# The first four blocks of a dynamic convolution and squared-ReLU network: 128-token chunks in block 0, and a new written order of the steps in blocks 0 to 3

## The chip, the cores and the metric

The kernel runs on one core of one Trainium2 chip. The metric is the device time of one execution in microseconds (us), from the first to the last instruction of that core. Lower is better.

## What is computed

The inputs are x (8 batches, 4096 tokens, 192 channels), weight_gen (for each token, 8 heads and 7 taps), and the two matrices w_in (192 x 2048) and w_out (2048 x 192) of a feed-forward network. The core of the reference is:

```python
w = softmax(weight_gen, over the 7 taps)
x_pad = 6 zero tokens ahead of each batch, then x
out[b, s, h, g] = sum over k of w[b, s, h, k] * x_pad[b, s + k, h, g]   # 24 channels g per head
h = maximum(out.reshape(32768, 192) @ w_in, 0)
result = (h * h) @ w_out
```

## The kernel before

**Blocks.** The 32768 tokens are 64 sub-blocks of 512 tokens. Blocks 0 and 1 hold one sub-block each, blocks 2 to 32 hold two. The two halves of a block, for one sub-block each 256 tokens, use the upper and the lower 64 rows of the TensorE array: 192 channels are three slices of 64.

**The steps.** In the code and in this text they have short names:
- *Softmax* (L131 to L235): a part of a batch's weights is loaded (`load`, L173), ACT takes the exponent (`exp`, L195), DVE sums over taps, takes the reciprocal and multiplies (L202, L209, L217), giving v. Small parts (8 tokens per partition) go to `v_first`, the others to `v_big`. `move_rows` then copies v's rows by DMAs from SP and POOL into `wr` tiles (L308), one small DMA for each of five token tiles; later parts go through DRAM (`vd`).
- *Band* (`st_band`, L326): DVE multiplies the rows with a mask, which gives for each of five token tiles a banded matrix `bd`.
- *Conv* (`st_conv`, "C"): TensorE multiplies x with the bands (L394, tiles of 32 columns of the array) into PSUM tiles `yp`; ACT copies them as fp16 into `y` (L405). The order of the matmuls comes from `conv_pieces`.
- *Unit* (`st_unit`, "u"): 12 matmuls of 64x256 (blocks 0 and 1, two slices of 128 hidden features) or 6 of 64x512 into one PSUM tile `h` (L419); ACT takes the ReLU into `t1` (L428), DVE squares it into `g` (L431). Block 0 and 1 have 8 units, the others 16.
- *Second matmul* ("M", `st_mm2`, L453): one M is half of the hidden features (8 of 16 chunks) for a quarter of 256 tokens. It sums in the PSUM banks `o`. After a quarter's second M, ACT copies `o` to `o_sb` (L467); where two banks were used (quarters of block 2 and later), DVE adds the second bank (L469). SP stores two quarters at a time (L474).

**What sets the order.** The program order is written by hand, and each engine runs its own instructions in that order. For each block a string gives the order on TensorE (`orders`, L558): block 0 "uuuuuCuuu", block 1 "MuMuuuMuuuMCu", block 2 "MuuuuMuuuuMuuuuuuuMCu", then `steady`, three times "MuMuuu" and then "MuuuMCu". The M steps in block j belong to block j - 1, C is the conv of block j + 1. Exponents, the rest of the softmax, bands and loads are hung on units by a table (`fill`, `TIMES`, `at`), and run just ahead of the unit (`run_fill`). x of blocks 2 and on is loaded by POOL (`x_load`) at the end of a block.

**Pools.** The PSUM tiles of conv, units and the warm-up share three buffers (`ps_h`); the `o` banks have one buffer each (`ps_o`). There are five `t1`, so the sixth ReLU waits for the first square. x has two fp16 buffers, bands three, rows four.

**The opening** (L506 to L554). TensorE spins on 42 warm-up matmuls. SP loads the first weights, w_in's two halves (`w_st`) and x of block 0 (`x_st`). ACT and DVE make the first softmax, and ACT casts w_in and x. SP and POOL move rows for block 0 (token tiles in the order 0, 2, 1, 4, 3, on the two in turn) and POOL those of block 1. `cross_w_in` copies each half of w_in across partitions by two SP DMAs (L126). Then follow x of block 1, the load of the second softmax part (s1), the bands of block 0, conv(0), the bands of block 1, and the cast of x(1) on DVE. A one-element POOL memset on `x_st` (L550) stands ahead of POOL's four loads of w_out (`load_w_out`, L139), so that these wait until x(1) has been cast; behind them stand the load of s2 and a memset of `v_big` (L554).

Of the kernel before, what the change touches and what calls it, by code (L numbers as in the profile page):

```python
# [9 lines left out]
def kernel(  # L10
# [7 lines left out]
):  # L18

# [279 lines left out]
    def wr_load_sbuf(j, parts, order, engines):  # L299

        wr_t[j] = p_wr.tile([P, NT, HP, SL * 2], f16, name="wr")
        n = 0
        for i in order:
            t0 = max(j % NBB * TB + tile_start(j, i), 0)
            for s in parts:
                a, b = max(t0, s.t0), min(t0 + P, s.t0 + P * s.r)
                if a < b:
                    engines[n % len(engines)].dma_start(  # L308
                        out=wr_t[j][a - t0 : b - t0, i].rearrange("p g c -> p (g c)"),
                        in_=s.v[  # L310
                            (a - s.t0) // s.r : (b - s.t0) // s.r, HALO : HALO + s.r
                        ].rearrange("p r g c e -> p r (g c e)"),
                    )
                    n += 1
# [33 lines left out]
    def conv_pieces(j):  # L348


        s0, n = BLOCKS[j]
        th = n * TB // 2
        halves = []
        for half in (0, 1):
            s, a = (s0 + half, 0) if n == 2 else (s0, th * half)
            halves.append([
                (s, i, half, max(bounds[i], a), min(bounds[i + 1], a + th), a)
                for i in range(NT) if bounds[i] < a + th and bounds[i + 1] > a
            ])
        if n == 2:  # L360
            for k in range(NK):
                for later in (True, False):
                    for pair in zip(*halves):
                        for s, i, half, a, b, base in pair:
                            for q in (2 * k, 2 * k + 1):
                                yield later, s, i, q, half, a, b, base
        else:
            for pair in zip(*halves):
                for later in (True, False):
                    for k in range(NK):  # L370
                        for s, i, half, a, b, base in pair:
                            for q in (2 * k, 2 * k + 1):
                                yield later, s, i, q, half, a, b, base

    def st_conv(j):

        n = BLOCKS[j][1]
        th = n * TB // 2
        per = 1024 // th
        y = p_y.tile([P, NK, TB], f16, name="y")  # L380
        y_t[j] = y
        yps = [
            ps_h.tile([P, 2 * TB], f32, name="yp", tag="h") for _ in range(-(-NK // per))
        ]
        for later, s, i, q, half, a, b, base in conv_pieces(j):
            lo = bounds[i]
            hi = lo + (STEP if tile_start(s, i) == starts[i] else bounds[i + 1] - lo)
            _, ha, hb, pre = quads[q]
            m, h = (32, hb) if later else (pre, ha)
            bd = bd_t[s][:, H * lo : H * hi].rearrange("p (g c e) -> p g e c", g=HP, e=2)  # L390
            p0 = RT * half + 32 * (q % 2)
            k = q // 2
            col = th * (k % per) - base
            nc.tensor.matmul(  # L394
                out=yps[k // per][p0 : p0 + m, col + a : col + b],
                lhsT=x_t[s][:, i, 32 * q : 32 * q + m],
                rhs=bd[:, h // 2, h % 2, a - lo : b - lo],
                start=True,
                stop=True,
                skip_group_check=True,  # L400
                tile_position=(0, p0),
            )
        for n, yp in enumerate(yps):
            k0, k1 = n * per, min((n + 1) * per, NK)
            nc.scalar.copy(  # L405
                out=y[:, k0:k1, 0:th],
                in_=yp[:, 0 : (k1 - k0) * th].rearrange("p (k c) -> p k c", c=th),
            )

    def st_unit(j, u):  # L410

        th = BLOCKS[j][1] * TB // 2
        per = TB // th
        h = ps_h.tile([P, 2, TB], f32, name="h", tag="h")
        for jj in range(per):
            for slot in range(NK):
                for half, r0 in enumerate((0, RT)):
                    k = slot ^ half if slot < 2 else slot
                    nc.tensor.matmul(  # L419
                        out=h[:, half, jj * th : (jj + 1) * th],  # L420
                        lhsT=w_in_chunk(u * per + jj, slot, half),
                        rhs=y_t[j][r0 : r0 + RT, k, 0:th],
# [7 lines left out]
        g_t[(j, u)] = g  # L430
# [4 lines left out]
    def new_o(pool, banks=2):  # L435
        if pool is ps_o:
            return [ps_o.tile([P, TB], f32, name=f"o{i}") for i in range(banks)]
# [3 lines left out]
    def st_mm2(j, qt, fcs, ccs, o):  # L441


        th = BLOCKS[j][1] * TB // 2
        per = TB // th
        half, off = divmod(qt * QT, th)
        for fc in fcs:
            g = g_t[(j, fc // per)][:, half, fc % per * th + off :]
            for cc in ccs:
                n = P // len(o)  # L450
                for i, oo in enumerate(o):
# [3 lines left out]
                        lhsT=g[r0 : r0 + n, cc * P : (cc + 1) * P],  # L455
# [32 lines left out]
    with nc.allow_low_precision("fp16 matmul pipeline"), tc.manual_schedule():  # L488
# [32 lines left out]
        spin(42)  # L521
        band_mask()
# [13 lines left out]
        wr_load_sbuf(0, [s0], (0, 2, 1, 4, 3), (nc.sync, nc.gpsimd))  # L536
        wr_load_sbuf(1, [s0], range(NT), (nc.gpsimd,))
        cross_w_in(0)
        x_cast(0, nc.scalar.copy)
        x_load_f32(1)  # L540
# [3 lines left out]
        for i in (0, 2, 1, 3, 4):  # L544
            st_band(0, (i,))
        st_conv(0)
        st_bands(1)
        x_cast(1, nc.vector.tensor_copy)

        nc.gpsimd.memset(x_st[1][:, 0:1], 0.0)  # L550
# [3 lines left out]
        nc.gpsimd.memset(v_big, 0.0)  # L554
# [3 lines left out]
        orders = {0: "uuuuuCuuu", 1: "MuMuuuMuuuMCu", 2: "MuuuuMuuuuMuuuuuuuMCu"}  # L558
        steady = "MuMuuu" * 3 + "MuuuMCu"

# [4 lines left out]
        def at(j, u, kind, *args):  # L565
# [5 lines left out]
            (0, 2): ((1, 7), (2, 0)),  # L571
            (0, 3): ((2, 15), (3, 0)),
# [8 lines left out]
        def exp_time(j, u):  # L581

            if u == 0:
                return j - 1, 5 if j == 2 else 12
            return j, {1: 0, 7: 3, 9: 4, 15: 8}[u]

        at(0, 4, "exp", s1, 0, s1.rh)
        at(0, 5, "soft", s1, 0, s1.rh)
        for n, s in enumerate(parts[2:], 2):
# [5 lines left out]
            pieces = [(lo, min(lo + PIECE, s.rh)) for lo in range(0, s.rh, PIECE)]  # L595
            for (j, u), (lo, hi) in zip(times, pieces, strict=True):
                at(*exp_time(j, u), "exp", s, lo, hi)
                at(j, u, "soft", s, lo, hi)
            if n > 2:
                at(times[0][0] - 1, 0, "load", s)  # L600
        for j in range(1, NBLK - 1):
            a = BLOCKS[j + 1][0]
            small = [p for p in parts if p.fb <= j + 1][-1].r == FIRST
            us = {1: (1, 3), 2: (6, 8), 6: (7, 9)}.get(j, (5, 9) if small else (1, 5))
            for n, u in enumerate(us):
                at(j, u, "band", a + n)
# [14 lines left out]
        def run_fill(j, u):  # L621
            for kind, *args in fill.get((j, u), ()):
                if kind == "band":
                    st_bands(*args)
                    continue
                if kind == "load":
                    args[0].load(nc.sync)
                    continue
                s, lo, hi = args
                if kind == "exp":  # L630
                    s.exp(lo, hi)
                    continue
                s.total(lo, hi)
                s.recip(lo, hi)
                s.scale(lo, hi, nc.vector)
                if hi < s.rh:
                    continue
                if s.r == FIRST:
                    move_rows(s)
                    after = parts[parts.index(s) + 1]  # L640
                    if after.b == s.b and after.r > FIRST:
                        s.store(nc.sync)
                else:
                    s.store(nc.sync)
                    stored.add(s)
                    for w in [w for w in waiting if w[0] is s]:
                        waiting.remove(w)
                        load_rows(w[1])

        FCS = (range(NF // 2), range(NF // 2, NF))  # L650
        for j, (sub, n) in enumerate(BLOCKS):
            if j + 2 < NBLK:
                load_rows(j + 2)
            u = m = 0
            for step in orders.get(j, steady):
                if step == "M":
                    qt, part = divmod(m, 2)
                    m += 1
                    if part == 0:
                        o = new_o(ps_o, 1 if j < 3 else 2)  # L660
                    st_mm2(j - 1, qt, FCS[part], (0, 1), o)
                    if part == 1:
                        o_sum(j - 1, qt, (0, 1), o)
                        if qt % 2:
                            o_store(j - 1, qt - 1, range(4), nc.sync)
                elif step == "u":
                    run_fill(j, u)
                    st_unit(j, u)
                    u += 1
                elif j + 1 < NBLK:  # L670
                    st_conv(j + 1)
            if j == 0:
                x_load(2)
                x_load(3)
            elif j < NBLK - 2:
                for k in range(BLOCKS[j + 2][0], sum(BLOCKS[j + 2])):
                    x_load(k)
# [47 lines left out]
```

The softmax here doesn't subtract the row's maximum and nothing guards it: scores larger than these inputs give would overflow.

## Time and profile before

| | |
|---|---|
| three runs | 749.04, 749.24 and 750.09 us, median 749.24 |
| span of the profiled execution | 749.2 us, granted clock 1.000 |
| ReLU, `t<-h` (L428) | 512 times, 1027 ns each on ACT |
| square, `g<-t` (L431) | 512 times, 687 ns each on DVE |
| second matmul (L453) | 8032 matmuls |
| units (L419) | 3168 matmuls |
| a block of 1024 tokens in the steady part | 22.55 us |
| w_out DMAs (L139) | four, from 18.75 us, 5.4 us each from issue to landing |
| load of s1 (L173) | issued by SP at 14.39 us |

A row of the profile's order of time reads: start in us, duration in us, engine, line, operation, output and input with their sizes, how many times; in brackets the idle time of the engine just before, and who ended it. A row with a count merges neighbours of one kind. A row of busy time by stretches reads: the stretch, its length, and for PE (matmuls), PEld (weight loads), DVE, ACT and POOL the busy us with the number of instructions; then the granted clock, the share of time that the DMA engines were busy (overlapping packets can take it over 1) and GB/s. SPq, ACTq and POOLq are queues' issue times of DMAs.

### The profile page before, as it was taken

What the parts mean: (1) busy time and instruction counts of PE and PEld (TensorE: products, weight loads), DVE (VectorE), ACT (ScalarE), POOL (GpSimd) and SP (SyncE); (2) the same over time, 40 slices, a digit from 0 to 9 for tenths busy, and PEclk for the clock granted to TensorE, in tenths of its full rate; (3) what the DMA queues carried; (4) which work ended last, traced back from release to release, by engine and by line L of the source; (5) the groups of instructions that cost most, each with busy time, mean ns of one, the idle gap of its engine ahead of it and who ended that gap; (6) DMA issues with size and microseconds to landing.
All of it is one profiled execution on the core that took longest, in us unless ns stands there. A gap on an engine that the chain in (4) does not pass through costs nothing.

```text
span 749.2 us, 33282 instructions
## 1 busy us (share of the span) xinstructions
PE 739.0 (99%) x15106; PEld 559.8 (75%) x15106; DVE 621.8 (83%) x1001; ACT 623.0 (83%) x753; POOL 87.9 (12%) x127
## 2 busy tenths in 40 slices
PE   8899999999999999999999999999999999999998
PEld 4658777777887777777877777777778777777787
DVE  5889998998789888887888888898888987677853
ACT  4898888888888888888888888888888888888883
POOL 3522220001101000011000110001100011001000
PEclk9999999999999999999999999999999999999999
DMA  8846444446453344543245442365441354441312
GB/s 231 129 74 135 79 68 109 101 78 138 93 109 69 74 77 80 131 86 65 46 80 139 86 80 49 55 138 108 59 79 47 57 109 80 59 75 50 50 45 65
DMA packets 122329, 65.20 MB, mean 87 GB/s; under 512 B 83881, under 2 KB 118668, under 8 KB 121676
## 3 DMA queue, kind: packets, MB, share of 16 engines
q1 hardware_dynamic: 77868, 46.05, 22.4%
q0 software_dynamic: 44176, 16.93, 20.6%
q8 instruction: 118, 1.93, 1.1%
q14 instruction: 23, 0.19, 0.1%
q10 hardware_dynamic: 144, 0.10, 0.0%
HBM read 48.61 MB, written 28.70 MB: 103 GB/s over the span
## 4 chain that ended last, share of the span: by engine, by line
PE 88%; DVE 5%; DMA 3%; ACT 1%; issue 1%; SPq 0%; POOL 0%; DVEq 0%; ACTq 0%
PE o L453 42%; PE h L419 40%; PE yp L394 6%; DVE g L431 2%; DVE bd L326 1%; DMA xt<-in_x_dram 1%; ACT t L428 1%; DMA x_st<-in_x_dram 1%; DMA vd<-v_big 1%; DVE v_first L217 1%; DVE ssum L202 0%; DVE rcp L209 0%; DMA wg<-in_weight_gen_dram 0%; DVE o_sb L469 0%; POOL wr L308 0%
## 5 line engine op out<-in xcount | busy, mean ns | idle before, releaser
L428 ACT ACTIVATE t<-h 128x1024 f16<-128x1024 f32 x512 | 497.1, 1027 | 66.9 <-PE h L419 66.6
L431 DVE TENSOR_TENSOR g<-t 128x1024 f16<-128x1024 f16 x512 | 334.5, 687 | 101.9 <-ACT t L428 99.1
L453 PEld LDWEIGHTS <-g 64*128 64x128 f16 (+1 forms) x8032 | 353.0, 94 | 55.7 <-issue 5.0
L453 PE MATMUL o<-w_o,g 64*128 64x192 f16 (+1 forms) x8032 | 386.1, 243 | 1.7 <-DMA w_o<-in_moe_w_out_dram 0.7
L419 PE MATMUL h<-y,w_i 64*128 64x512 f16 (+1 forms) x3168 | 379.8, 370 | 2.1 <-ACT t L428 0.9
L419 PEld LDWEIGHTS <-w_i 64*128 64x128 f16 x3168 | 165.5, 94 | 114.7 <-issue 5.0
L326 DVE TENSOR_TENSOR bd<-wr,mask 128x4160 f16<-128x4160 f16 (+3 forms) x89 | 149.4, 1702 | 4.6 <-DMA wr<-v_first 4.6
L278 POOL DMA_DIRECT2D xt<-in_x_dram x62 | 51.3, 832 | 446.1 <-PE yp L394 422.8
L467 ACT COPY o_sb<-o 128x384 f32<-128x384 f32 x129 | 62.3, 483 | 33.2 <-PE o L453 33.2
L469 DVE TENSOR_TENSOR o_sb<-o,o_sb 128x384 f32<-128x384 f32 x123 | 68.2, 554 | 8.0 <-ACT o_sb L467 5.6
L405 ACT CAST y<-yp 128x1024 f16<-128x1024 f32 (+1 forms) x64 | 48.2, 803 | 16.5 <-PE yp L394 16.5
L394 PE MATMUL yp<-bd,xt 128*32 128x104 f16 (+8 forms) x3864 | 52.0, 208 | 1.8 <-DMA xt<-in_x_dram 1.2
L394 PEld LDWEIGHTS <-xt 128*32 128x32 f16 (+3 forms) x3864 | 46.1, 91 | 8.0 <-issue 6.4
L217 DVE TENSOR_TENSOR v_big<-ex,rcp 128x112 f16<-128x112 f32 (+1 forms) x136 | 27.3, 263 | 1.8 <-DMA vd<-v_big 0.6
L195 ACT ACTIVATE ex<-wg 128x448 f32<-128x448 f32 (+2 forms) x44 | 27.2, 618 | 1.9 <-DMA wg<-in_weight_gen_dram 1.9
L202 DVE TENSOR_REDUCE ssum<-ex 128x64 f32<-128x448 f32 (+2 forms) x44 | 26.1, 593 | 2.4 <-ACT ex L195 2.4
L209 DVE RECIPROCAL rcp<-ssum 128x64 f32<-128x64 f32 (+2 forms) x44 | 23.7, 539 | 1.5
L268 POOL DMA_DIRECT2D xt<-in_x_dram x7 | 3.8, 547 | 136.9 <-PE yp L394 136.9
L308 POOL DMA_DIRECT2D wr<-v_first x31 | 16.8, 562 | 15.4 <-DVE v_first L217 15.3
L516 PE MATMUL wp<-warm 128*128 128x512 f16 x42 | 11.1, 432 | 1.3 <-DVE warm L508 1.3
L516 PEld LDWEIGHTS <-warm 128*128 128x128 f16 x42 | 4.5, 109 | 7.4 <-issue 2.5
L217 DVE TENSOR_TENSOR v_first<-ex,rcp 128x112 f16<-128x112 f32 (+1 forms) x48 | 9.1, 255 | 0.3
(19 smaller groups left out, 24.5 us busy)
## 6 DMA issues: line engine op xcount, KB each, us to landing
out_dram<-o_sb SPq DMA_DIRECT2D x63, 384.0 KB, 2.9
xt<-in_x_dram POOLq DMA_DIRECT2D x42, 240.0 KB, 6.0
wg<-in_weight_gen_dram SPq DMA_DIRECT2D x4, 1064.0 KB, 7.7
xt<-in_x_dram POOLq DMA_DIRECT2D x20, 192.0 KB, 5.6
wr<-vd SPq DMA_DIRECT2D x38, 80.0 KB, 5.0
vd<-v_big SPq DMA_DIRECT2D x5, 512.0 KB, 5.5
wg<-in_weight_gen_dram SPq DMA_DIRECT2D x5, 392.0 KB, 4.2
wg<-in_weight_gen_dram SPq DMA_DIRECT2D x3, 616.0 KB, 5.5
```

Source lines behind the costliest of these rows:

```text
L195: nc.scalar.activation(out=self.ex[:, lo:hi].rearrange("p r g k e -> p (r g) k e"), in_=self.wg[:, lo:hi].rearrange("p r (g e) k -> p (r g ...
L217: eng.tensor_tensor(out=bass.AP(tensor=v.tensor, offset=v.offset + lo * H * SL + lo % SL * 2 + g * SL * 2, ap=[list(v.ap[0]), [H * SL + 2, ...
L278: eng.dma_start(out=dst[:, first:last], in_=ap)
L326: nc.vector.tensor_tensor(out=bd_t[j][:, H * lo : H * (lo + len(tiles) * n)].rearrange("p (g m c) -> p g m c", g=shape[1], c=2 * SL), in0= ...
L394: nc.tensor.matmul(out=yps[k // per][p0 : p0 + m, col + a : col + b], lhsT=x_t[s][:, i, 32 * q : 32 * q + m], rhs=bd[:, h // 2, h % 2, a - ...
L405: nc.scalar.copy(out=y[:, k0:k1, 0:th], in_=yp[:, 0 : (k1 - k0) * th].rearrange("p (k c) -> p k c", c=th),)
L419: nc.tensor.matmul(out=h[:, half, jj * th : (jj + 1) * th], lhsT=w_in_chunk(u * per + jj, slot, half), rhs=y_t[j][r0 : r0 + RT, k, 0:th], ...
L428: nc.scalar.activation(out=t1, in_=h, func=ActF.Relu)
L431: nc.vector.tensor_tensor(out=g, in0=t1, in1=t1, op=AluOp.mult)
L453: nc.tensor.matmul(out=oo[:, cc * Dm : (cc + 1) * Dm], lhsT=g[r0 : r0 + n, cc * P : (cc + 1) * P], rhs=w_o[r0 : r0 + n, fc, :], start=(fc ...
L467: nc.scalar.copy(out=o_sb, in_=o[0][:, c])
L469: nc.vector.tensor_tensor(out=o_sb, in0=o[1][:, c], in1=o_sb, op=AluOp.add)
```

## The change

- **Block 0 by chunks.** Its four chunks of 128 tokens go to the halves in turn: chunks 0 and 2 to the upper, 1 and 3 to the lower half (`place`, `spans`). Conv(0) has two parts of two chunks each, each with its own y copy of 128x384. Its first four units take one part only, and four slices of 128 features (`unit_span`): units 0 and 1 do features 0 to 1023 for part 0, units 2 and 3 for part 1, with 24 matmuls of 64x128 each. Units 4 to 7 are as before. Conv(0) has 96 matmuls instead of 72.
- **The opening.** The memset of `v_big` is POOL's first work. Rows of block 0 go in the order 0 to 4: tiles 0 to 2 on SP and POOL in turn, 3 and 4 on POOL. Rows of block 1: tiles 0 to 2 by ACT's queue, after the cast of x(0), 3 and 4 by POOL. Bands of block 0 are made in the order 0 to 4. The POOL memset on `x_st` is gone, so the loads of w_out and s2 follow the rows directly. x(2) is loaded right after conv(0)'s second part, x(3) right after conv(1).
- **The order of blocks 0 to 3** is written out with all kinds of steps: u, M, c (second part of conv(0)), C, B (bands of a sub-block), X (cast of x), E (one piece of an exponent), S (the rest of its softmax), L (load of a part). Blocks 4 and on keep `steady` and their table.
- **The banks.** M steps are numbered through by a generator, so they can stand in any block. For quarters of blocks 0 and 1, which use one bank, `o0` and `o1` now alternate.

```diff
+        nc.gpsimd.memset(v_big, 0.0)
         band_mask()
...
-        wr_load_sbuf(0, [s0], (0, 2, 1, 4, 3), (nc.sync, nc.gpsimd))
-        wr_load_sbuf(1, [s0], range(NT), (nc.gpsimd,))
+        wr_load_sbuf(0, [s0], (0, 1, 2), (nc.sync, nc.gpsimd))
+        wr_load_sbuf(0, [s0], (3, 4), (nc.gpsimd,))
         cross_w_in(0)
         x_cast(0, nc.scalar.copy)
+        wr_load_sbuf(1, [s0], (0, 1, 2), (nc.scalar,))
+        wr_load_sbuf(1, [s0], (3, 4), (nc.gpsimd,))
...
-        for i in (0, 2, 1, 3, 4):
+        for i in range(NT):
             st_band(0, (i,))
-        st_conv(0)
-        st_bands(1)
-        x_cast(1, nc.vector.tensor_copy)
-
-        nc.gpsimd.memset(x_st[1][:, 0:1], 0.0)
+        st_conv(0, 0)
         for q in range(4):
             load_w_out(q, 4)
         s2.load(nc.gpsimd)
-        nc.gpsimd.memset(v_big, 0.0)
-        orders = {0: "uuuuuCuuu", 1: "MuMuuuMuuuMCu", 2: "MuuuuMuuuuMuuuuuuuMCu"}
         steady = "MuMuuu" * 3 + "MuuuMCu"
+        plans = {
+            0: "B1 c u u u X1 u E1 S1 u u u M C u",
+            1: "L3 u B2 B3 u u u M u u E2 S2 M u E2 C S2 u M",
+            2: "L4 u u u E3 M u u u M B4 u u u u M B5 u u u S3 u M u E3 C u",
+            3: "L5 L6 M S3 u u u M u B6 u u E4 u M M B7 u u u u E4 M M u S4 C u M u u M u",
+        }
...
+    def unit_span(j, u):
+        if j == 0 and u < 4:
+            return range(u % 2 * 4, u % 2 * 4 + 4), u // 2 * P, P
...
-                        o = new_o(ps_o, 1 if j < 3 else 2)
+                    o = new_o(ps_o, 1, qt % 2) if j < 2 else new_o(ps_o)
...
+                elif kind == "c":
+                    st_conv(0, 1)
+                    x_load(2)
+                elif kind == "C" and j + 1 < NBLK:
+                    st_conv(j + 1)
+                    if j == 0:
+                        x_load(3)
```

## The prediction

> **What bounds the kernel now.** I read the page first, then the table of busy time by stretches, then the order of time of the first 62 us with its waits.
>
> ```profile
> PE 739.0 (99%) x15106; PEld 559.8 (75%) x15106; DVE 621.8 (83%) x1001; ACT 623.0 (83%) x753; POOL 87.9 (12%) x127
> ```
>
> TensorE looks full over the whole span, so only its stretches can tell where time is left. The next lines give, for each stretch, its length and the busy time of PE, PEld, DVE, ACT and POOL.
>
> ```profile
> 11.40:14.10 2.70, 2.21 (x55) 1.06 (x54) 2.60 (x5) 1.29 (x1) 1.05 (x3) 1.00 0.90 213
> 14.10:20.83 6.73, 5.75 (x167) 4.94 (x166) 5.51 (x7) 5.29 (x7) 2.18 (x4) 1.00 0.68 179
> 20.83:30.00 9.17, 7.45 (x108) 5.86 (x103) 7.06 (x17) 6.97 (x10) 7.84 (x11) 1.00 0.96 149
> 30.00:40.30 10.30, 9.06 (x222) 7.50 (x216) 9.35 (x16) 8.41 (x12) 2.86 (x5) 1.00 0.71 129
> 40.30:53.60 13.30, 13.02 (x122) 6.74 (x122) 11.88 (x18) 12.39 (x16) 3.11 (x6) 1.00 0.52 80
> 53.60:61.50 7.90, 7.90 (x224) 6.26 (x222) 7.76 (x18) 6.90 (x10) 2.23 (x3) 1.00 0.49 87
> 61.50:66.70 5.20, 5.06 (x88) 3.78 (x84) 3.86 (x10) 4.01 (x6) 2.72 (x5) 1.00 0.61 83
> 66.70:80.59 13.89, 13.89 (x315) 11.55 (x312) 13.39 (x19) 12.72 (x17) 0.29 (x1) 1.00 0.39 104
> 80.59:103.14 22.55, 22.55 (x476) 16.61 (x474) 21.77 (x43) 20.04 (x27) 4.74 (x9) 1.00 0.37 67
> ```
>
> From 80.59 us, the first second-matmul step of block 4, a block takes 22.55 us and PE has no idle time. Blocks 4 to 32 keep their order, so **what is won by 80.59 is won at the end, and no more**. Up to there no engine is full; the waits are these:
>
> ```profile
> 15.47 3.88 PE L419 MATMUL h<-y,w_i 64*128 64x256 f16 x60 [0.89 <-ACT y L405]
> 21.89 1.52 PE L419 MATMUL h<-y,w_i 64*128 64x256 f16 x24 [0.90 <-ACT t L428]
> 24.14 1.48 PE L453 MATMUL o<-w_o,g 128*128 128x192 f16 x16 [0.72 <-DMA w_o<-in_moe_w_out_dram]
> 36.65 1.58 PE L394 MATMUL yp<-bd,xt 128*32 128x104 f16 x118 [1.05 <-DMA xt<-in_x_dram]
> ...
> 14.57 2.36 DVE L326 TENSOR_TENSOR bd<-wr,mask 128x3328 f16<-128x3328 f16 x2 [0.48 <-DMA wr<-v_first]
> 17.47 0.66 DVE L292 CAST xt<-x_st 128x960 f16<-128x960 f32 x1 [0.54 <-DMA x_st<-in_x_dram]
> 21.87 0.69 DVE L431 TENSOR_TENSOR g<-t 128x1024 f16<-128x1024 f16 x1 [1.04 <-ACT t L428]
> 29.23 2.33 DVE L326 TENSOR_TENSOR bd<-wr,mask 128x4160 f16<-128x4160 f16 x1 [1.00 <-DMA wr<-v_first]
> 40.30 0.69 DVE L431 TENSOR_TENSOR g<-t 128x1024 f16<-128x1024 f16 x1 [0.88 <-ACT t L428]
> ```
>
> The bracket is idle time before the instruction. Three floors say how much there is to win by the first M of block 4:
> - **DVE**: its first band starts at 11.49; the eight stretches sum to 2.60+5.51+7.06+9.35+11.88+7.76+3.86+13.39 = 61.4 us busy. Floor 11.5+61.4 = 72.9.
> - **PE**: 48 units at 0.647 (18 matmuls, three units, in 1.94 in the chain of waits), 16 M at 1.32 (32 in 1.32 there), five convs about 6.2 (0.9, 0.9 and three near 1.5): 58.4. From 12.3: 70.7.
> - **ACT**: relus 0.915 apart (three in 2.85 with a tail of 1.02), so 48 cost 43.9; y copies about 6, o copies 8 x 0.48, exps about 4.3: 58. From a first copy at 13.8, plus 0.9 for the first unit: 72.7.
>
> So VectorE and ScalarE bound this stage nearly as closely as PE, and **DVE's 80.6 - 72.9 = 7.7 us of idle time is the sum to share out**.
>
> **What the Trainium skill says.** "TensorE: Matmul & The Clock Gate", section Back-to-back issue gap, gives N/2.4 + 2.5 ns warm, and a sustained 81 ns at N=128 with a weight load each. Our pairs of 512 columns agree with the first (1.94/9 = 216 ns). The second doesn't fit packed halves: 32 matmuls of 64x192 with 32 loads take 1.32, 41 ns each. The same page, Architectural detail, calls ACT and DVE strict FIFO: the waits above are all in program order, which agrees. "DMA: Bandwidth & Descriptors", Issuing engines are not separate DMA queues, says that SP, ACT and POOL issues share the same 16 DMA engines; its section on queues has an engine take rings in turn by packets. No run here shows how two queues share.
>
> **The change, part by part.**
> 1. *Conv of block 0 in two parts.* Part 0 needs bands 0 to 2 alone; the third band starts at 12.50 and takes 0.58. Its last 24 matmuls go out at 13.15 to 13.5, y copy (128x384, 0.48 as the o copy) at 13.8 to 14.3, against 14.62 to 15.42 now. Part 1 follows band 4 (ends 14.09), done about 14.5. First unit at 14.5, first relu about 15.3 instead of 16.34: **1.0 us earlier on ACT**. Added: 24 matmuls (13 ns each, 0.3, in PE's wait for bands) and about 0.2 of ACT copy.
> 2. *Four units of 24 matmuls x 128 columns in place of 12 x 256.* No such row before. Low end 12 pairs x 55.8 (skill) = 0.67, high end 24 x 41 (the 64x192 row; a narrower one is not dearer) = 0.99. ACT needs 0.915 per unit, so it hides the low end; the high end costs 0.3 + 4 x 0.08 = 0.6. I take 0.1.
> 3. *Rows of block 1.* Five DMAs leave SP's and POOL's queues for three on ACT and two on POOL. Three ACT issues at 0.37 (ACT's one at the end) to 0.6 (SP's) take 9.6 to at most 11.5; behind them stands the second w_i cast, which waits for data until 11.22 anyway: 0 to 0.3, and it feeds only unit 4. SP is freed of one 0.6 issue, so x_st(1) leaves 0.6 sooner, and the 0.54 wait of its cast goes. POOL issues 5 instead of 7, so DVE's 0.48 wait goes.
> 4. *v_big memset* (2.5 us) to POOL's start: the mask is ready near 6.2, needed at 11.49; nothing. It leaves POOL's 22.3 to 24.8, where no one waited.
> 5. *w_o and s2 loads* lose the wait for x_st(1) (POOL idle 5.79) and follow five row issues: 11.4 instead of 18.75. The 0.72 wait on w_o goes. But 1.5 MB now runs beside the crossing of w_i (issued at 13.04, wanted by unit 4 near 18.9) and the s1 load (issued at 14.39). w_o's landing is 5.4 us, moving from about 1.7 after issue. The exp of s1 stands on ACT ahead of the fifth relu, wanted near 19.0. Low end: no delay. High end: the queues halve each other from 13 us on; what took HW transfers until 18.5 takes until 22, delay 3.0. Packets of the w_i and s1 transfers are far larger than w_o's, so turns by packet favour them: I take **0.8**.
> 6. *Order of block 0 and 1.* x(2) is loaded after conv part 1, x(3) after conv(1), behind POOL's five rows of S1, not at the end of the block (28.78): x(3) at about 26 to 27.6, landing near 33 by the 6 us in the issue table; conv(2) is wanted near 32. That ACT wait is absorbed, as DVE is then behind with S2. The first M moves into block 0. S1 now runs at 20 to 23.2 (0.96+0.85+1.46) instead of 22.5 to 25.8, its rows land 3.4 later (25.82 to 29.23 now), at 26.6, before DVE asks for bands 2 at 27: the 1.00 wait goes. The 0.21+1.04 before g of units 3 and 4 go, as bands and cast are ahead of them or hidden. First relu of block 2 comes near 37 instead of 41.2, so DVE's 0.88 goes too.
> 7. *Blocks 2 and 3.* The same steps, the same number of M by each block's start (4, 8, 16). The 3.5 us of DVE idle left there shrink where DVE carries a backlog: 0 to 2.0, I take 0.5. New waits: bands of block 6 follow S3 closely (0 to 1.0, take 0.5); block 3 ends "M u" and block 4 starts with M on the same two o banks, so PE waits for copy and sum (0.3+0.48+0.55) behind one unit of 0.65: 0 to 0.75, take 0.3, since part of it falls on DVE's wait. Alternating banks before that is free: M's there stand two or more units apart.
>
> Sum of removed DVE idle: 0.48+0.54+1.25+1.00+0.88 = 4.15; plus 0.5; minus 0.8, 0.5, 0.1, 0.3: **gain 2.95 us**. The profiled span is 749.2, the median of the runs 749.24: 746.2.
>
> **Rivals.**
> - *Nothing collides*: the w_o term is 0 and the backlog fills 2.0 of the later idle time: 4.15+2.0-0.9 = 5.2, 744.0. For it: HW transfers at 14 to 18 us ran at 160 to 350 GB/s, so they weren't always full.
> - *Collision*: delay 3.0 at the exp of s1, everything behind it on DVE (S1, bands 2 and 3) shifts: 2.95-2.2 = 0.75, 748.5.
> - *Given back*: block 3's bunched M M meet a DVE backlog; sums of o come late, PE waits on its banks; about 1.5 more lost: 747.7. For it: DVE is 21.77 of 22.55 full even in steady state.
> - *Slower*: the exp of s1 blocks ACT's queue. Break-even is where it starts 2.95+0.8 = 3.75 after 19.0, at 22.8; over 0.2% slower needs 24.3. At 25.5 the total is 751.9. Against it: that landing would take 10 us, the longest in the first 40 us is 6.5.
>
> **Chances.** My forecast (745 to 747.6) 0.45, nothing collides 0.22, given back 0.12 (half of it within 0.2%), collision 0.13, slower 0.08. Within 0.2% (1.5 us) is what a measurement here can't tell from no change. Faster 0.45+0.22+0.06 = 0.73, same 0.06+0.13 = 0.19, slower 0.08. The range runs from "nothing collides" to past the collision, 744.0 to 749.0.
>
> **What would show it.** Right: first relu near 15.3; no wait on w_o; PE's conv(2) ends by 35; the first M of block 4 near 77.6; block 4 on still 22.55. Step 5 wrong: ACT idle before the exp of s1, or PE idle on w_i, over 1 us. Step 2 wrong: units 0 to 3 over 0.95 apart on PE with ACT waiting. Step 7 wrong: PE waits on "DVE o_sb" in block 3. A block after the fourth that isn't 22.55 would break the whole argument.

## The result, and the profile after

The changed kernel is **slower**: median 754.3 us (752.69 to 755.27, four runs) against 749.66 us (749.04 to 750.46, four runs) on the same chip, ratio 1.0059 [1.0037, 1.0081]. A later repeat (c0_after below) gave 1.0027 [1.0016, 1.0038]. The forecast was 746.2 us, range 744.0 to 749.0.

The page of the changed kernel points to the causes. First the busy time of the engines, then three of its costliest groups; the last column is the idle time just before the group and what ended most of it.

```profile
PE 740.0 (98%) x15178; PEld 560.7 (74%) x15178; DVE 622.5 (83%) x1001; ACT 623.7 (83%) x754; POOL 86.6 (11%) x124
...
L477 PE MATMUL o<-w_o,g 64*128 64x192 f16 (+1 forms) x8032 | 384.0, 243 | 2.1 <-DVE o_sb L493 1.9
L441 PE MATMUL h<-y,w_i 64*128 64x512 f16 (+2 forms) x3216 | 380.2, 369 | 5.4 <-issue 3.3
...
L196 ACT ACTIVATE ex<-wg 128x448 f32<-128x448 f32 (+2 forms) x44 | 27.1, 615 | 4.3 <-DMA wg<-in_weight_gen_dram 4.3
```

```profile
L195 ACT ACTIVATE ex<-wg 128x448 f32<-128x448 f32 (+2 forms) x44 | 27.2, 618 | 1.9 <-DMA wg<-in_weight_gen_dram 1.9
```

The last row is the exponents of the kernel before. The instructions do the same work: 72 matmuls more, one copy more on ACT, 1 us more of PE time. What has grown are waits: 1.9 us of second matmuls on the sum of `o_sb` in VectorE, 3.3 us of units on "issue" (nothing that the profile names), and 4.3 us of exponents on the load of weights, where there were 1.9. Next, where they stand: rows of the order of time of the changed kernel, then two of the kernel before.

```profile
15.98 2.85 ACT L450 ACTIVATE t<-h 128x1024 f16<-128x1024 f32 x3 [0.30 <-PE h L441]
20.94 0.98 PE L441 MATMUL h<-y,w_i 64*128 64x128 f16 x13 [3.27 <-issue]
23.45 0.39 PE L441 MATMUL h<-y,w_i 64*128 64x256 f16 x1 [1.53 <-DMA w_i<-w_i]
25.23 0.93 ACT L196 ACTIVATE ex<-wg 128x784 f32<-128x784 f32 x1 [2.47 <-DMA wg<-in_weight_gen_dram]
...
70.30 2.33 DVE L328 TENSOR_TENSOR bd<-wr,mask 128x4160 f16<-128x4160 f16 x1 [2.27 <-DMA wr<-v_first]
74.95 2.80 PE L477 MATMUL o<-w_o,g 64*128 64x192 f16 x63 [1.46 <-DVE o_sb L493]
85.94 1.48 PE L477 MATMUL o<-w_o,g 64*128 64x192 f16 x31 [0.46 <-DVE o_sb L493]
```

```profile
16.34 3.77 ACT L428 ACTIVATE t<-h 128x1024 f16<-128x1024 f32 x4 [0.92 <-PE h L419]
19.97 0.96 ACT L195 ACTIVATE ex<-wg 128x784 f32<-128x784 f32 x1
```

The first ReLU does start earlier, at 15.98 instead of 16.34. Then TensorE stands still from 17.67 to 20.94, waits again for `w_i`, and ACT starts the exponent of s1 at 25.23 instead of 19.97. In block 3 VectorE waits 2.27 us for rows before a band, and PE waits 1.46 and 0.46 for a sum that VectorE owes. The next rows are two stretches and one single microsecond of the changed kernel (columns as before: PE, PEld, DVE, ACT, POOL, granted clock, DMA share, GB/s).

```profile
15.10:20.94 5.84, 2.57 (x90) 2.40 (x86) 3.92 (x5) 3.33 (x4) 0.63 (x1) 1.00 1.09 212
...
62.17:85.29 23.12, 21.66 (x445) 15.43 (x442) 19.75 (x35) 18.86 (x24) 5.94 (x10) 1.00 0.54 102
...
21.00:22.00 1.00, 0.92 (x13) 0.54 (x12) 0.00 (x0) 0.26 (x1) 0.00 (x0) 0.50 1.33 244
```

From 15.10 to 20.94 PE works 2.57 us of 5.84, where its stretch before (14.10 to 20.83) had 5.75 of 6.73. After the standstill TensorE's clock is at half for 6.8 us, from 21.0 to 27.8, so that the wait is paid once more in slow matmuls. "TensorE: Matmul & The Clock Gate", section What's actually happening, in the Trainium skill puts this drop after at least one idle window of about 3.4 us. The 3.27 us here are nearly that; in other runs (last section) the clock fell after less, and there the measurement decides.

To see what each stretch lost, take PE's start of the first unit of block 2, the first unit of block 3, and the first second-matmul step (M) of block 4, in the profiled runs. d4_gate and d1_again are experiments described below.

| start on PE, us | before | after | d4_gate | d1_again |
|---|---|---|---|---|
| block 2, first unit | 40.35 | 42.74 | 38.15 | 37.82 |
| block 3, first unit | 58.98 | 62.17 | 57.59 | 57.27 |
| block 4, first M | 80.59 | 85.25 | 80.56 | 78.49 |
| span | 749.2 | 753.6 | 749.1 | 746.5 |

From the last of these to the end it is 668.6 us before and 668.4 after (749.2 - 80.59 and 753.6 - 85.25), so the rule of the forecast holds: what is won or lost by block 4's first M is won or lost at the end. The row of block 2 doesn't hold the same work everywhere: in the kernel before, five M stand ahead of that unit, in the other three only four, and an M there takes 1.43 us of TensorE (38.92 to 40.35). With this M counted in, the 4.66 us lost are 3.8 by block 2 and 1.47 in block 3, and block 2 itself gives 0.6 back.

### The profile page after: what moved, and what is told of

Read it like the earlier page. It is cut to its first block, busy times and chain, and to the rows that moved or that the text cites. A ratio compares the mean times of both kernels' runs of the same rounds, so it can differ in the third digit from the quotient of the medians.

```text
span 753.6 us, 33423 instructions
## 1 busy us (share of the span) xinstructions
PE 740.0 (98%) x15178; PEld 560.7 (74%) x15178; DVE 622.5 (83%) x1001; ACT 623.7 (83%) x754; POOL 86.6 (11%) x124
## 3 DMA queue, kind: packets, MB, share of 16 engines
q8 instruction: 118, 1.93, 1.0%
## 4 chain that ended last, share of the span: by engine, by line
PE 95%; DMA 2%; DVE 1%; ACT 1%; SPq 1%; issue 0%; ACTq 0%
PE o L477 45%; PE h L441 44%; PE yp L408 6%; DMA w_i<-w_i 1%; DMA w_st<-in_moe_w_in_dram 1%; DVE g L457 1%; ACT t L450 0%; DVE bd L328 0%; SPq L120 0%; DVE o_sb L493 0%; ACT w_i L568 0%; SPq L118 0%; ACT y L419 0%; SPq L269 0%; SPq L127 0%
## 5 line engine op out<-in xcount | busy, mean ns | idle before, releaser
L441 PE MATMUL h<-y,w_i 64*128 64x512 f16 (+2 forms) x3216 | 380.2, 369 | 5.4 <-issue 3.3
L419 ACT CAST y<-yp 128x512 f16<-128x512 f32 (+2 forms) x65 | 48.3, 792 | 15.7 <-PE yp L408 15.6
L408 PE MATMUL yp<-bd,xt 128*32 128x104 f16 (+7 forms) x3888 | 52.1, 208 | 1.6 <-DVE bd L328 1.5
```

What stands on the lines that cost most here:

```text
L408: nc.tensor.matmul(out=yps[k // per][p0 : p0 + m, col + a : col + b], lhsT=x_t[s][:, i, 32 * q : 32 * q + m], rhs=bd[:, h // 2, h % 2, a - ...
L419: nc.scalar.copy(out=y_t[j][:, k0:k1, col0 : col0 + w], in_=yp[:, 0 : (k1 - k0) * w].rearrange("p (k c) -> p k c", c=w),)
L441: nc.tensor.matmul(out=h[:, half, jj * w : (jj + 1) * w], lhsT=w_in_chunk(fc, slot, half), rhs=y_t[j][r0 : r0 + RT, k, col : col + w], sta ...
```

## Experiments

Ratios are to the kernel before on the same chip, with 95% intervals. They fall into three questions.

### Do the early loads of w_out cost the opening?

**a1_gate** keeps the whole change but makes POOL's loads of w_out and s2, and that of x(2) behind them, wait for x(1) to land: a one-element copy of x(1) stands ahead of them (the gate). **b1_early** does the opposite in the kernel before: the memset that held these loads back is left out. **c0_after** is the changed kernel again.

```diff
+ a1_gate:   junk = const.tile([P, 1], f32, name="junk")
+ a1_gate:   nc.gpsimd.tensor_copy(out=junk, in_=x_st[1][:, 0:1])
- b1_early:  nc.gpsimd.memset(x_st[1][:, 0:1], 0.0)
             for q in range(4):
                 load_w_out(q, 4)
```

> The changed kernel, with one small POOL copy of a column of x(1) ahead of the w_out loads, so that these (and s2 and x(2) behind them) wait for x(1)'s landing again; all else as changed. Collision (the early w_out, s2 and x(2) loads hold up SP's transfers): x(1), the crossing of w_i and s1 land 4 to 6 us after issue instead of about 10, TensorE's idle 3.3 us at 17.7 and its halved clock go, 745 to 748 us. Small matmuls (24 per unit, 72 more instructions starve TensorE's queue): the 3.3 us idle in unit 3 stays, above 752 us.

> The kernel before, without the one-element POOL memset that makes the w_out loads wait for x(1); all else as before, no small matmuls. Collision: x(1), w_i crossing and s1 land late here too, TensorE idles several us near 18 to 22, 752 to 756 us. Small matmuls: nothing happens, 749 to 750 us, or a little faster as the 0.72 us wait on w_out goes.

> The changed kernel once more, to compare on one chip with its variants. Ratio to the kernel before as measured first, 1.004 to 1.008. Both theories: TensorE idles 3 to 4 us in unit 3 with no wait that the profile names.

a1_gate: 0.9999 [0.9989, 1.0009]; b1_early: 1.0021 [1.0013, 1.0030]; c0_after: 1.0027 [1.0016, 1.0038]. So with the gate nothing is left of the loss, and early loads alone slow the kernel before by 0.21%, 1.6 us. No run parts w_out from s2, which moves with it. a1_gate was expected at 745 to 748 us and came to 751.45: the half clock went, but 1.86 us of the unnamed idle stayed, and so did block 3's waits on `o_sb` (1.08 and 0.46 us). c0_after was expected at 1.004 or more. The views of DMA issues up to 30 us tell how. The last number is the median time from issue to landing; first the changed kernel, then a1_gate.

```profile
x_st<-in_x_dram SPq DMA_DIRECT2D x2, 384.0 KB, 9.9
w_i<-w_i SPq DMA_DIRECT2D x4, 192.0 KB, 10.4
w_o<-in_moe_w_out_dram POOLq DMA_DIRECT2D x4, 192.0 KB, 10.9
```

```profile
x_st<-in_x_dram SPq DMA_DIRECT2D x2, 384.0 KB, 4.7
w_i<-w_i SPq DMA_DIRECT2D x4, 192.0 KB, 4.4
w_o<-in_moe_w_out_dram POOLq DMA_DIRECT2D x4, 192.0 KB, 5.1
```

In this profile every transfer in flight together takes about twice as long, SP's as well as POOL's; in c0_after they took 7.6, 9.1 and 10.6 us, in b1_early 7.3, 5.1 and 9.7. There was little room for more: in the kernel before, the DMA engines were busy 0.93 to 1.06 of the time from 15 to 18 us. One of these microseconds:

```profile
15.00:16.00 1.00, 0.53 (x10) 0.53 (x11) 1.00 (x1) 0.42 (x1) 0.00 (x0) 1.00 1.03 349
```

b1_early shows the price on ACT, and c0_after one on TensorE, in the order of time:

```profile
22.87 0.94 ACT L195 ACTIVATE ex<-wg 128x784 f32<-128x784 f32 x1 [2.45 <-DMA wg<-in_weight_gen_dram]
```

```profile
21.79 3.95 PE L441 MATMUL h<-y,w_i 64*128 64x128 f16 x47 [4.54 <-issue]
```

In b1_early the exponent of s1, at 19.97 in the kernel before, leaves ACT idle for 2.45 us; TensorE waits 1.62 and 1.23 us for `w_i`, and its clock is at half for 6.8 us. In c0_after, the changed kernel once more, neither of these data waits is left: the unnamed idle alone, 4.54 us, is longer than both. So the same traffic costs different waits in different executions.

### What does block 3's new order cost?

**a3_plan3** puts back block 3's old order (M steps apart, S at its old place), **c2_gate_p3** does so with the gate. **d1_again** and **e3_pair** are c2_gate_p3 in two later comparisons; **d4_gate** is a1_gate beside d1_again on one chip.

```diff
-  3: "L5 L6 M S3 u u u M u B6 u u E4 u M M B7 u u u u E4 M M u S4 C u M u u M u",
+  3: "M S3 L5 L6 u M u u u M u M B6 u u u M E4 u M B7 u u u M E4 u u u M C S4 u",
```

> The changed kernel, with block 3 in the order it had before (MuMuuu three times, MuuuMCu, with its loads, bands and softmax pieces where they hung). If block 3's bunched M steps cost what the trace shows (1.46 and 0.46 us of TensorE waiting for the sum of o, 2.3 us of VectorE waiting for rows): 1.5 to 2 us less than the changed kernel, 752 to 753 us, and no wait of TensorE on the sum of o. If that wait only takes the place of another: within 0.5 us of the changed kernel.

> The changed kernel with the w_out loads behind x(1)'s landing, small matmuls kept, block 3 in its order of before. Theory that block 3's bunched M steps cost 1.7 us (M of block 4 came 23.3 us after the first unit of block 3, against 21.6 before): ratio to before 0.997 to 0.998. Rival (a wait only moves on): ratio 0.999 to 1.001.

> The changed kernel with w_out's loads gated behind x(1)'s landing and with block 3 in its old order, a second time. If the two losses (early loads of w_out, bunched second matmuls of block 3) are real and add up: ratio to before 0.993 to 0.997, first second-matmul step of block 4 near 79.1 us. If the first result was a lucky chip: 0.998 to 1.001, and step of block 4 near 80.5.

> The changed kernel with the gate alone (as in a1_gate), on the same chip as d1_again. If block 3's written order costs 1.7 us in itself: 0.2 to 0.5% slower than d1_again, TensorE waits of 0.5 to 1.5 us on the sum of o_sb at the end of block 3 and the start of block 4. If not: the same as d1_again.

> d1_again once more, on the chip of e2_late: ratio to before 0.995 to 0.997, idle after about 85 unit matmuls of 0 to 2 us.

a3_plan3: 1.0004 [0.9993, 1.0016]. c2_gate_p3: 0.9948 [0.9930, 0.9967]; d1_again: 0.9967 [0.9955, 0.9978]; e3_pair: 0.9960 [0.9948, 0.9973]. d4_gate: 0.9999 [0.9988, 1.0010]. Gate and old order together **beat the kernel before** in three comparisons, by 0.33 to 0.52%, and c2_gate_p3 beat the changed kernel on one chip (c0_after, 1.0027); the same kernel without the old order (d4_gate, same chip as d1_again) does not. a3_plan3, at 752.0 us, came where its first theory had it, with no wait on `o_sb`. In the table above d4_gate and d1_again reach block 3 within 0.32 us of each other, then d4_gate takes 22.97 us to block 4's first M and d1_again 21.22. All profiles agree: this stretch takes 22.42 to 23.38 us in the six with the new order and 21.22 to 21.74 in the nine with the old one. The rows of d4_gate's order of time say why; the last is the same band in d1_again:

```profile
65.70 2.33 DVE L328 TENSOR_TENSOR bd<-wr,mask 128x4160 f16<-128x4160 f16 x1 [2.25 <-DMA wr<-v_first]
...
70.35 2.80 PE L477 MATMUL o<-w_o,g 64*128 64x192 f16 x63 [1.44 <-DVE o_sb L493]
81.25 1.48 PE L477 MATMUL o<-w_o,g 64*128 64x192 f16 x31 [0.45 <-DVE o_sb L493]
```

```profile
65.65 2.32 DVE L328 TENSOR_TENSOR bd<-wr,mask 128x4160 f16<-128x4160 f16 x1
```

VectorE, strictly in program order, stands 2.25 us at the bands of block 6, since their rows were only just sent; so it does the squares and sums behind them late, and two M steps in a row ask for a bank whose sum is still queued (it runs from 69.75 to 70.30, TensorE goes on at 70.35). In d1_again, where one unit and two M more lie between the softmax and these bands, and no two M stand together, neither wait is there.

Units 0 to 15 of block 2 seemed to lose 0.8 us (19.45 us in d1_again, 18.63 before). **d2_spread** tests whether that is the same thing: d1_again with one M after every four units there.

```diff
-  2: "L4 u u u E3 M u u u M B4 u u u u M B5 u u u S3 u M u E3 C u",
+  2: "L4 u u u E3 u M u u u u M B4 u u u u M B5 u u S3 u M E3 C u",
```

> d1_again with block 2's first three units ahead of its first second-matmul step put further apart: u, then M after every four units. If the spacing in block 2 costs what the traces suggest (units 0 to 15 of block 2 take 19.4 us against 18.6 before): 0.8 us less by block 4's first step, ratio 0.1% below d1_again. If that time is lost to VectorE, which has more work queued there than before, the order is worth nothing: within 0.05% of d1_again and the 19.4 us stay.

0.9956 [0.9940, 0.9973] against d1_again's 0.9967 [0.9955, 0.9978] on one chip: not told apart, and block 2 took 19.79 us in its profile (20.82 in c3_all, which has this order too), not less than d1_again's 19.45. The profiles show no gain from the spacing. Two rows of busy time for block 2, the kernel before and then d1_again:

```profile
40.35:58.98 18.63, 18.35 (x297) 11.08 (x298) 17.17 (x27) 17.77 (x22) 4.67 (x9) 1.00 0.44 79
```

```profile
37.82:57.27 19.45, 19.45 (x314) 12.12 (x314) 19.03 (x37) 18.72 (x24) 4.36 (x8) 1.00 0.47 96
```

There was no loss to find. The stretch of d1_again holds 17 matmuls more: the M (16 of them, 1.43 us) that before stood ahead of block 2's first unit. Without it the stretch would be 0.6 us shorter than before, although VectorE has 1.86 us more work in it and ACT 0.95. Block 3 is 0.39 us shorter too. A stretch between two marks is to be compared only after its instructions are counted.

### What is the idle time that no wait names?

**a2_whole** leaves block 0 as it was before (one conv, units of 256 columns) in the changed kernel; **c1_gate_whole** does so with the gate; **c3_all** with the gate, block 3's old order, and block 2's M after every four units.

```diff
  def place(j, c):
-     if j == 0:
-         return c % 2, c // 2 * P
      return divmod(c * P, BLOCKS[j][1] * TB // 2)
```

> The changed kernel, with block 0's conv in one part and its units of 12 matmuls x 256 columns as before; early loads, queues and the written order stay. Collision: within 1.5 us of the changed kernel, 753 to 756 us, TensorE still idle near 18 to 22. Small matmuls: the idle goes, 746 to 750 us.

> The changed kernel with the w_out loads behind x(1)'s landing, and block 0's conv and units whole (12 matmuls x 256 columns). With the loads held back but the small matmuls kept, TensorE still idled 1.86 and 0.96 us with no wait named, 128 matmuls apart (256 instructions), each time 1.4 us after a 16 KB packet on the instruction queue ended. Theory instruction fetch (small matmuls use up the fetched instructions faster than the next 16 KB comes in beside the loads): both idles shrink or go, first relu 0.6 us later, 1 to 2.5 us less than with the small matmuls, ratio to before 0.997 to 0.999. Rival (those idles belong to the loads alone, not to the number of matmuls): the idles stay, and the time is the same or 0.6 us longer, ratio 1.000 to 1.001.

> The changed kernel with all three undone: w_out loads behind x(1), block 0 whole, block 3 in its order of before; and block 2's M steps after every four units. What stays of the change: the queues of the rows, the early x(2) and x(3), M in block 0, S1 and bands earlier, alternating banks. If the losses add up as read from the traces (collision 4.4, fetch 2, block 3 1.7, block 2 up to 0.8 us, against the changed kernel): ratio to before 0.993 to 0.996. If they hide each other: 0.998 or more.

a2_whole 1.0030 [1.0019, 1.0041], c1_gate_whole 0.9997 [0.9986, 1.0009], c3_all 0.9975 [0.9966, 0.9984]. In a2_whole, where the unnamed idle should have gone or stayed near 18 to 22, the named waits take over (PE 3.37 and 0.93 us on `w_i`, ACT 4.25 us on the load of s1), and the time is that of c0_after: with the loads early, the opening waits for data whichever way block 0 is cut. With whole units no kernel has an unnamed idle among the first four units. But from the first band to the first ReLU a whole conv takes 4.85 us (a2_whole, c3_all) where the two parts take 3.91, and c1_gate_whole is no faster than a1_gate, against an expected 0.1 to 0.3%. Its profile can't say more: its bands came late and its clock was at half from 14.6 to 21.4. c3_all, expected at 0.993 to 0.996 if the losses added up, comes out above c2_gate_p3 (0.9948) on the same chip, though the intervals just touch; its profile has 20.82 us in block 2, where c2_gate_p3 has 19.45. So this idle is not shown to be a cost that adds to the others.

What it is, **d3_warm** shows; **e2_late** was to show it from the other side. Both are d1_again with another warm-up of TensorE: 84 matmuls of 256 columns instead of 42 of 512 (84 more instructions, weight loads counted, the same time), or 24 that start after the first exponent (36 fewer). **e1_fewer** meant to take fewer as well, by 21 fp32 matmuls.

```diff
  d3_warm:  out=wp[:, 0 : TB // 2], lhsT=warm[:, 0:P], rhs=warm[:, 0 : TB // 2]   spin(84)
  e1_fewer: out=wp[:, 0:256], lhsT=warm32[:, 0:P], rhs=warm32                    spin(21)
  e2_late:  after s0.exp: nc.scalar.copy(out=warm[:, 0:1], in_=warm[:, 1:2])     spin(24)
```

> d1_again with the warm-up in 84 matmuls of 256 columns in place of 42 of 512: the same TensorE time, 84 more instructions ahead of the first conv. If the unnamed idle of TensorE among the first four units is an instruction packet that has not landed, it sits at a fixed count of instructions and moves forward by 42 matmuls, from after about 85 unit matmuls to after about 43 (or shows up once more, 128 matmuls apart). If it has to do with the data, the buffers or the work of unit 3, it stays after about 85. Ratio within 0.2% of d1_again either way.

> d1_again with the warm-up in 21 matmuls of fp32 (256 columns each) in place of 42 of f16: fewer TensorE instructions ahead of the first conv, 21 fused ones where the order of the program shows 42 weight loads and 42 matmuls before, that is 63 fewer. If the unnamed idle is an instruction packet at a fixed count of instructions, it moves back by about 31 unit matmuls, from after 85 to after about 116, and is shorter by the time that these take (about 1 us) or gone. If it depends on the data or on unit 3, it stays after 85. The fp32 warm-up's length is not known; it should end between 9 and 13.5 us, or the conv starts late or the clock falls.

> d1_again with a warm-up of 24 matmuls that starts 4 us later (after the first exponent) in place of 42: 36 TensorE instructions fewer ahead of the conv. If the unnamed idle is an instruction packet at a fixed count of instructions, it moves back by 18 unit matmuls, from after about 85 to after about 103, and is shorter by what these take (0.5 us of matmuls, up to one ReLU) or gone; on the total 0 to 0.15% below e3_pair. If it has to do with the data or with unit 3, it stays after about 85 and the total is that of e3_pair. Should the clock not be up by the conv, the conv and units 0 and 1 take twice as long, and it shows in the granted clock.

First the rows of d4_gate, where the idle is at its usual place, then d3_warm, then e1_fewer:

```profile
14.56 2.57 PE L441 MATMUL h<-y,w_i 64*128 64x128 f16 x85
18.25 2.49 PE L441 MATMUL h<-y,w_i 64*128 64x128 f16 x47 [1.11 <-issue]
```

```profile
14.85 1.40 PE L441 MATMUL h<-y,w_i 64*128 64x128 f16 x43
19.63 6.32 PE L441 MATMUL h<-y,w_i 64*128 64x128 f16 x89 [3.39 <-issue]
```

```profile
1.27 12.26 PE L540 MATMUL wp<-warm 128*128 128x256 f32 x42 [1.27 <-DVE warm L532]
...
19.02 2.46 PE L441 MATMUL h<-y,w_i 64*128 64x128 f16 x47 [1.71 <-issue]
```

With 42 more pairs of load and matmul ahead, the idle moves from after 85 unit matmuls to after 43: exactly 42. It sits at a **count of instructions**, not at a place in the work. Counted from the first warm-up matmul, it comes after 223 matmuls in all nine profiles that have it (42 + 96 + 85, in d3_warm 84 + 96 + 43). e1_fewer doesn't contradict this: each fp32 matmul shows up as two (42 in the row), so the count was the same and the idle stayed. Its one time was 747.74 us beside 751.24 for the kernel before. e2_late has no such idle at all, but that proves nothing: neither has d1_again, whose packet (below) came at 15.2 (its 99 unit matmuls run through). In a1_gate a second one of 0.96 us follows exactly 128 matmuls after the first (47 of units, 16 of M, 65 of conv), 256 instructions. c3_all, with whole units, has none after 223, but it has this one, also after 351 matmuls:

```profile
28.85 1.07 PE L471 MATMUL o<-w_o,g 128*128 128x192 f16 x11 [0.46 <-issue]
```

The page's DMA queues have one called "instruction": 118 packets, 1.93 MB, so about 16 KB each. The kernel before has 15106 matmuls and as many weight loads, and 118 packets too: 256 instructions to a packet. In steps of 0.2 us, the first packet of that queue after 12 us starts at 18.6 to 19.8 in the five profiles with early loads, when SP's and POOL's loads fill the engines, and at 15.2 to 17.2 in the kernel before and the eleven with the gate. TensorE goes on about 0.8 to 1.7 us after its end each time. So TensorE had run out of instructions, and the early loads delayed these too.

In the total the idle could not be sized: e2_late 0.9965 [0.9953, 0.9977], e3_pair on its chip 0.9960 [0.9948, 0.9973], whose profile has 0.52 us of it. The profile of e2_late is of the slowest of its seven runs: the first band came late, conv(0) started at 13.49, and the clock was at half from 15.9 to 19.3 us. The same happened in the profile of d2_spread, whose warm-up is unchanged, so it isn't shown to be the price of the later warm-up. d3_warm came to 0.9982 [0.9971, 0.9992], 0.15% over d1_again; its profile, with 3.39 us of idle, is of a run 2.5 us above its median.

## Why the prediction was wrong

- **Step 5 failed: the term of w_out's early loads.** It took 0.8 us with 3.0 as the high end, because larger packets would be favoured, because the transfers of 14 to 18 us, at 160 to 350 GB/s, seemed to leave room, and because no landing had taken over 6.5 us. In the run, `w_i` took 10.4 instead of 4.0 us, w_out 10.9 instead of 5.4: the larger packets were not favoured. And GB/s was a poor measure of room: the DMA engines were busy 0.93 to 1.06 of the time at 15 to 18 us already. The exponent of s1 started at 25.23, ACT idle for 2.47 us before it and PE for 1.53 on `w_i`: both of the forecast's signs that step 5 is wrong. The forecast's "slower" rival had named this very mechanism and priced a start at 25.5 with 751.9 us; it got a chance of 0.08 on the argument that such a landing would be too long. That argument came from a trace in which w_out's loads came after the others, so it had nothing to say about an overlap. Against the gate it costs 0.28% (c0_after against a1_gate, each to its own chip's kernel before) to 0.6% (first comparison): about 2 to 4.5 us.
- **Step 5 had no term for what follows a wait**: half a clock for 6.8 us, and the instruction packet that shares the DMA engines (3.27 us of idle).
- **Step 7 failed in size**: 0.3 us for bunched M and 0.5 for bands of block 6. With the gate, block 3's order costs 1.75 us in the traces (22.97 against 21.22) and 0.32% (2.4 us) in the runs of one chip. The mechanism was in the rival "given back", with 1.5 us; the trace adds its start, the band that waits for rows at the head of VectorE's queue. The forecast's sign for it, PE waiting on `o_sb` in block 3, came with 1.46 us. The 0.5 us of idle to be won in blocks 2 and 3 is there once the order is undone: d1_again takes 0.6 us less for block 2 (the moved M counted) and 0.39 less for block 3.
- **Step 2, half right.** A part unit needs more time on PE than 0.647 us (85 matmuls in 2.57 us, so 24 take 0.73), but ACT hid it at full clock, as taken (three ReLUs in 2.85 us, as before); at half clock, in d3_warm and d2_spread, they stand about 1.28 us apart. Not seen was that 72 extra matmuls are 144 extra instructions.
- **Step 1, right.** The first ReLU came at 15.98, with the gate at 15.18 to 16.02 in c2_gate_p3, d4_gate, a1_gate and d1_again, forecast 15.3. The spread is that of the first band, at 11.27 to 12.07 in these runs. From the first band to the first ReLU it is 4.85 us before and 3.91 to 3.97 in all of these: 0.9 us won, forecast 1.0. In d2_spread and e2_late, with the first bands at 12.9 and the clock at half, the ReLU was at 17.64 and 17.38.
- **Step 6, half right where the loads are held back.** Conv(2) ran from 33.22 to 35.28 in d1_again (forecast: done by 35), block 2's first ReLU at 38.69 instead of 41.21 (forecast 37); but 1.43 of these 2.5 us are the M that now stands behind three units of block 2. The 1.00 us wait for the bands of block 2, forecast to go, is 1.18 there. **Steps 3 and 4** cost nothing that the traces show.
- **The frame held**: the 668 us after block 4's first M did not change, so every loss of the opening reached the end.

With steps 5 and 7 repaired, the rest of the change gives 0.33 to 0.52%, 2.5 to 3.9 us, where the forecast's own list without the terms of w_out and of block 3 (4.15 + 0.5 - 0.1) has 4.55; in the profiles of these runs block 4's first M comes at 78.49 to 79.10, 1.5 to 2.1 us earlier than before.

What stays open is how the loss splits between late data, late instructions and the slow clock: all three come with the same traffic, and none was changed alone. The granted clock of the single runs on the chip of c0_after says how closely the loss goes with the clock. Of 52 runs of the kernel before, 28 have 1.000, on average 751.9 us; 11 have 0.998 and take 752.7, three have 0.995 and take 754.3. Of 22 runs of the changed kernel none has 1.000; five have 0.998 and take 753.3, 14 have 0.995 and take 754.6. At equal clock it is only 0.2 to 0.7 us slower. This is no split by cause, since in the traces the clock falls after TensorE has stood idle.

## What to carry to other kernels

A wait that holds a load back may be the reason why the critical loads are quick: before moving a load earlier, list what is in flight then, read the busy share of the DMA engines and not their GB/s, and take at least twice the quiet landing time, as it was here, for the pessimistic case. In an in-order queue place a step by when its input lands, not by when its output is wanted: what stands behind it, a sum for PE here, pays. And when small instructions replace large ones, count the instructions, not only their busy time: here TensorE ran out of them, though what that cost in the total was not shown.

## What the runs showed of the hardware

- An idle on "issue" in TensorE sat at a fixed count of instructions (after 223 matmuls, and 256 instructions later), was 0.5 to 4.5 us long, and ended about 0.8 to 1.7 us after a 16 KB packet of the "instruction" DMA queue, which carries 256 instructions.
- 768 KB of w_out (four DMAs of 192 KB), with s2 and x(2) behind them, beside other loads doubled the landing in the changed kernel: `w_i` from 4.0 to 10.4 us, x from 5.1 to 9.9, w_out itself from 5.4 to 10.9.
- TensorE's clock fell to half after 1.95 us of idle in c2_gate_p3, and in e2_late after gaps none longer than 1.11 us (d2_spread: 1.03); not after one idle of 1.86 us in a1_gate or of 1.11 in d4_gate. "TensorE: Matmul & The Clock Gate", What's actually happening, asks for an idle window of about 3.4 us; these runs differ from it.
- Once it fell, the clock stayed at half for 3.4 us (a2_whole, c0_after, c2_gate_p3, d2_spread, e2_late) or for 6.8 (after, a3_plan3, b1_early, c1_gate_whole, d3_warm), and for no other length.

Rows for the clock: the idle of c2_gate_p3, then a stretch of e2_late with 0.50 as the granted clock while PE is busy throughout:

```profile
18.82 4.19 PE L441 MATMUL h<-y,w_i 64*128 64x128 f16 x47 [1.95 <-issue]
```

```profile
16.00:18.00 2.00, 2.00 (x42) 2.00 (x41) 1.72 (x2) 1.08 (x2) 0.00 (x0) 0.50 1.04 271
```
